# One attention-and-experts kernel: threshold searches over bf16 digits, closer row units, and two output tiles side by side

## Chip, cores and metric

The kernel runs on one NeuronCore of a Trainium2 chip, as one launch. The metric is device time in microseconds (us). The engines are named as the trace names them: PE (matrix products), DVE (VectorE), ACT (ScalarE), POOL (GpSimd), SP (DMA issue).

## What is computed

```python
# attention: q, k, v of [8, 8, 576, 64], tau = 0.02
scores = (q @ k.T) / sqrt(64)
scores = where(scores >= rowmax(scores) - tau, scores, -1e9)
x = softmax(scores) @ v                       # reshaped to [4608, 512]
# routing: 8 experts, 576 places each
flat = (x @ w_gate).flatten(); order = argsort(-flat)
for idx in order:                             # best (token, expert) pair first
    tok, e = divmod(idx, 8)
    if assigned[tok] >= 0 or counts[e] >= 576: continue
    assigned[tok] = e; counts[e] += 1
# experts
for e in range(8): out[assigned == e] = relu(x[assigned == e] @ w1[e]) @ w2[e]
```

## The kernel before

**Attention (0 to about 441 us).** The eight batches pass through scores, threshold softmax (on DVE line 75 takes the row maximum and line 91 applies it; POOL line 76 makes the bias `nb` between the two) and products with `v`. Two batches are also turned at the end: 30 *row units* (`xt_unit`, PE line 247, ACT lines 250 and 251, one DMA each) transpose a tile of `x` and send it to a table `xrows` in DRAM. They use two PSUM banks, `xo0` and `xo1`, in turn. The last loop of `attention` deals them out at a pitch `XTY` between the steps of the first search.

**Routing.** The greedy assignment is made one expert at a time: `Router.phase` finds the threshold at which the next expert fills its 576 places. The 4608 tokens lie as [128 partitions, 36 columns]; `prep` takes each token's best logit `b` and a one-hot of its expert `oh`. Then a *search* of seven steps narrows the threshold. One step is: `step_cmp` on DVE compares all 36 columns with 16 or 32 trial values (128x576 or 128x1152 results, `cmp`); `step_cnt` on PE counts them per expert in nine matmuls (line 500); the counts of four column blocks are added; `step_flag` on DVE (`jka`) sees which trial values still overfill; `step_n` on PE (line 549, later 535) sums the flags, and DVE makes the next trial values from the sum (`jk`, `E`, or `st` and `sd`). How the four blocks are added hangs on the search's number `count`: for 1 and 2 DVE copies (`cn`) and PE adds with four matmuls (line 519); for 3 DVE multiplies and reduces (`cm`, `c8n`) and PE adds with one matmul (line 517); above `ADDS=3` DVE copies and adds three times (`cs`).

After a search, `pick`, `rank1` and `pack` turn the threshold into a list of 576 rows (`gq`, `gx`, `scol`, `poh`, `th`, `R`, `ob`, `idx`; PE lines 591, 592, 619, 625), and POOL gathers these rows of `xrows` by indirect DMA (`xg`, line 798). Search 1 runs alone after attention; search r+2 runs inside the expert stage r.

**Experts (about 489 to 960 us).** Each stage is an FFN on PE in three-term f32r products (high and low parts): first products (line 884, eight tiles f of 128 hidden units, 12 matmuls for each half of the rows), then second products (line 916): five row tiles in the order `L2O=(0,4,1,2,3)`, each over f = 0 to 7. DVE makes the low part of each hidden tile (`H<-hf,H`), of the weights (`w1l`, `w2l`) and of the inputs (`xl`).

**Who sets the order.** All engines' queues are filled by a Python planner when the program is built. The class `Vec` (line 412) keeps an expected time for DVE: 0.07 us plus the elements at 0.96 per ns, or at 1.9 per ns for a `tensor_tensor` whose output and first input are bf16 (line 424, `twice`). PE's matmuls are dealt out at fixed expected pitches, and a step of the search is put into PE's queue when the planner expects DVE to be done. Low-priority DVE work (`H`, `w2l` and others) waits in a list `fills` and is pulled between search steps. Once the program runs, each engine goes through its queue in order and waits wherever the real time differs.

Of the kernel before, what the change touches and what calls it, by code (L numbers as in the profile page):

```python
# [19 lines left out]
PPB=8; LTB=1; VTB=4; HOLD=1; XW=520; NBO=2; NDEF=4; XTB=4; XTY=1.05; XT0=-1.2; XRB=2  # L20


def attention(ctx, tc, qk, vl, wgd, xrows, xts, Lg, nb_batches, ident, dup, idle, R, after_first):
    nc=tc.nc
# [273 lines left out]
    def tail():  # L298
# [89 lines left out]
NC_=36; J=32; CAP=576; BIGS=8192.0; RC=1.5*2.0**28; NH=20; ADDS=3  # L388

def const_arrays():  # L390

    k=np.zeros((128,4096),np.float32); o={}; pos=0
    def put(name,a):
        nonlocal pos
        a=np.asarray(a,np.float32)
        if a.ndim==1: a=np.broadcast_to(a,(128,a.size))
        k[:a.shape[0],pos:pos+a.shape[1]]=a; o[name]=(pos,a.shape[1]); pos+=a.shape[1]
    e=[2.0**(-126+16*i) for i in range(16)]
    put("E1",np.array([-FMAX]+[-x for x in reversed(e)]+e+[FMAX]))
    put("pw",np.array([2.0**i for i in range(J+2)])); put("nw",np.array([2.0**-i for i in range(J+2)]))  # L400
    put("lev",2.0**(1-5.0*np.arange(1,6)))
    lw=np.tile(2.0**(1-5.0*np.arange(1,6)),(128,1)); lw[0,4]=0; put("lew",lw)
    put("io",np.arange(J+2)); put("io4",np.arange(J+2)/16)
# [5 lines left out]
    put("eye",np.eye(128))  # L409
    return k[:,:pos].copy(),o  # L410
# [22 lines left out]
class Router:  # L433
# [8 lines left out]
    def setup(s,ident):  # L442
# [3 lines left out]
        s.eye=t("eyer",[128,128],F32R); V.tensor_copy(s.eye,ident)  # L446
# [5 lines left out]
        x=ident.rearrange("p (c t) -> p c t",c=4); V.tensor_reduce(s.own,x,axis=AX.X,op=ALU.add)  # L452
        with s.nc.allow_low_precision(reason="one term of each sum is not zero"): V.tensor_reduce(s.sum,x.rearrange("p c t -> p t c"),axis=AX.X,op=ALU.add)
    def consts(s):
        V=s.V; G=s.G
        t=lambda n,sh,dt:s.cp.tile(sh,dt,name=n)
        s.tri=t("trib",[128,128],BF16); V.scalar_tensor_tensor(s.tri,s.k("eye"),BIGS,s.k("tri"),op0=ALU.mult,op1=ALU.add)
# [3 lines left out]
        s.cmp=t("cmp",[128,NC_*J],BF16); s.fl=t("fla",[128,6],BF16); G.memset(s.fl,0.0)  # L461
# [49 lines left out]
    def step_flag(s,lv):  # L511
# [3 lines left out]
        else:  # L515
            n=s.ps()[0:32,0:8]
            if s.count>2: s.T.matmul(n,s.sum,s.cn,start=True,stop=True)
            else:
                for c in range(4): s.T.matmul(n,s.eye[:,32*c:32*c+32],s.cn[:,8*c:8*c+8],start=(c==0),stop=(c==3))
        if lv==1: V.tensor_scalar(s.st,s.st,s.lo,None,op0=ALU.add)  # L520
        jk=s.wk.tile([32,9],BF16,name="jka"); s.jk=jk; m=s.js
        fl=jk[:,8:9] if lv==5 else s.fl[0:m,lv+1:lv+2]
        V.tensor_scalar(jk[0:m,0:8],n[0:m],CAP-0.5,None,op0=ALU.is_ge,op1=ALU.max,accum_out=fl)
    def step_n(s,B):

        V=s.V
        lv=B["lv"]
        ps=s.ps()
        if lv>0:


            d=ps[:,0:1]
            for l in range(lv,0 if s.alone else lv-1,-1):
                k=32 if l==5 else 128
                s.T.matmul(d,s.hb[0:k,l-1:l].to_broadcast([k,128]),s.jk[:,8:9] if l==5 else s.fl[:,l+1:l+2],start=(l==lv),stop=(l==1 or not s.alone))
            if not s.alone and lv<5:
                sd=s.wk.tile([128,1],F32,name="sd",bufs=3)
                if lv==1: V.tensor_copy(sd,d)
                else: V.tensor_tensor(sd,B["add"],d,op=ALU.add)
                d=sd  # L540
            if lv<5: return {"add":d,"lv":lv+1}
            s.T.matmul(ps[:,1:10],s.ones[0:32],s.jk,start=True,stop=True)
            lo=s.wk.tile([128,1],F32,name="lo5",bufs=2)
            if s.alone: V.tensor_tensor(lo,s.lo,d,op=ALU.add)
            else: V.scalar_tensor_tensor(lo,d,B["add"],s.lo,op0=ALU.add,op1=ALU.add)
            return {"lo":lo,"lv":6,"full":ps}
        E2=s.wk.tile([128,J+2],F32,name="E",bufs=3)
        n=ps[:,0:1]
        s.T.matmul(n,s.ones,s.fl[:,lv+1:lv+2],start=True,stop=True)
        sm=s.wk.tile([128,2],F32,name="sm",bufs=3); lo=sm[:,0:1]  # L550
        jk=s.wk.tile([128,J+2],F32,name="jk2")
        V.scalar_tensor_tensor(jk,s.k("io"),n,B["E"],op0=ALU.is_equal,op1=ALU.mult,accum_out=lo)
        if lv==-1:

            V.tensor_scalar(E2,s.k("pw"),lo,FMAX,op0=ALU.mult,op1=ALU.min)
            V.scalar_tensor_tensor(E2,s.k("nw"),lo,E2,op0=ALU.mult,op1=ALU.max)
        else:
            s.ab=sm[:,1:2]
            V.scalar_tensor_tensor(s.ab,lo,-1.0,lo,op0=ALU.mult,op1=ALU.max)
            V.tensor_scalar(E2,s.k("io4"),s.ab,lo,op0=ALU.mult,op1=ALU.add)  # L560
        return {"E":E2,"lo":lo,"lv":lv+1}
# [19 lines left out]
    def rank1(s,E):  # L581
# [3 lines left out]
        V.scalar_tensor_tensor(gq[:,:NC_],s.b,lo,gm,op0=ALU.is_gt,op1=ALU.mult)  # L585
# [62 lines left out]
    def phase(s,last=False):  # L648
# [10 lines left out]
        if last:  # L659

            lo=s.wk.tile([128,1],F32,name="lo"); V.memset(lo,-FMAX/4); E={"lo":lo}
        else:
            E={"E":s.k("E1"),"lv":-1}
# [38 lines left out]
GA=[5.0,6.5,8.0,8.0]; AGE=7.0; HALF=1; WARM=[30,6,64]  # L702
W1Y=1.0; W1X=8.5; L2O=(0,4,1,2,3); L2Z=1; HFB=3; RW=[0.2,0.4,0.4,0.4]; LOWP=(); LPF=7; LOWT=1.4; PREPW=1; WLY=(1.0,1.0)

def moe(ctx,tc,R,start,xrows,w1,w2,out,ident):
# [11 lines left out]
    fills=[]  # L717
    def later(k,g): fills.append((clk[0],k,g))
    def pull(k=None):
        if fills:  # L720
            i=next((i for i,x in enumerate(fills) if x[1]==k),None)
            if i is None: i=next((i for i,x in enumerate(fills) if x[1][0] in ("hl","w2l","w2")),0)
            _,k,g=fills.pop(i); g(); done.add(k)
    R.fill=pull
    def flush():
        while True:
            if fills and (clk[0]-fills[0][0]>AGE or (not R.on and V.free<=clk[0]+0.2)): pull()
            yield 0.3

# [128 lines left out]
    def ffn(r,s):  # L858
        H=wk.tile([128,8,2*CAP],F32R,name="H")
        def want(*k):  # L860
            while k not in done:
                if any(x[1]==k for x in fills): pull(k)
                else: yield k

# [196 lines left out]
```

## Time and profile before

| | |
|---|---|
| three runs | 967.71 us median (966.82 to 968.75) |
| the profiled execution | 965.63 us, its span 963.9 us |
| PE busy | 936.5 us (97%) |
| DVE busy | 775.7 us (80%) |
| mean granted TensorE clock | 0.996 |

The span runs from the first to the last instruction of the profiled execution; the device time has 1.7 us around it. Busy shares are averages over stages with different limits, so they have to be read stage by stage. Of a row of the timeline the first number is the start, the second the duration; durations contain the time an instruction spends in the pipeline, so the pitch of a series is read from start to start.

### The profile page before, as it was taken

What the parts mean: (1) busy time and instruction counts of PE and PEld (TensorE: products, weight loads), DVE (VectorE), ACT (ScalarE), POOL (GpSimd) and SP (SyncE); (2) the same over time, 40 slices, a digit from 0 to 9 for tenths busy, and PEclk for the clock granted to TensorE, in tenths of its full rate; (3) what the DMA queues carried; (4) which work ended last, traced back from release to release, by engine and by line L of the source; (5) the groups of instructions that cost most, each with busy time, mean ns of one, the idle gap of its engine ahead of it and who ended that gap; (6) DMA issues with size and microseconds to landing.
All of it is one profiled execution on the core that took longest, in us unless ns stands there. A gap on an engine that the chain in (4) does not pass through costs nothing.

```text
span 963.9 us, 24282 instructions
## 1 busy us (share of the span) xinstructions
PE 936.5 (97%) x9182; PEld 700.8 (73%) x9182; DVE 775.7 (80%) x2177; ACT 638.3 (66%) x1301; POOL 277.7 (29%) x485
## 2 busy tenths in 40 slices
PE   7999999999999999998889999999999999999996
PEld 4565666566566656565778797897988979898994
DVE  8999999999999999996778787788897978536220
ACT  6999999999999999996645343443543525455430
POOL 3434354353534343340020302113041323310101
PEclk9999999999999999999999999999999999999999
DMA  6322252533432333205752505325342516530101
GB/s 260 124 101 88 85 195 93 205 127 111 168 111 101 125 102 123 88 2 193 251 181 74 191 18 173 107 90 175 105 154 94 168 49 215 183 103 32 39 12 44
DMA packets 36293, 117.02 MB, mean 121 GB/s; under 512 B 4304, under 2 KB 4944, under 8 KB 35664
## 3 DMA queue, kind: packets, MB, share of 16 engines
q1 hardware_dynamic: 28784, 93.89, 27.9%
q0 software_dynamic: 5888, 19.03, 6.3%
q10 hardware_dynamic: 1504, 2.54, 0.9%
q8 instruction: 73, 1.20, 0.5%
q14 instruction: 44, 0.36, 0.1%
HBM read 93.01 MB, written 21.38 MB: 119 GB/s over the span
## 4 chain that ended last, share of the span: by engine, by line
PE 84%; DVE 7%; issue 5%; DMA 2%; POOL 0%; ACT 0%; POOLq 0%; ACTq 0%; DVEq 0%
PE pf L884 19%; PE pf L916 18%; PE sc L70 15%; PE xo L156 14%; PE tb L99 9%; PE sc L99 2%; PE xo L166 2%; PE pt L825 1%; DVE cmp L429 1%; DVE z L75 1%; DVE pp L91 1%; PE rps L500 1%; DMA out_dram<-y,idx 1%; PE xo L178 1%; DMA xg<-xrows,idx 1%
## 5 line engine op out<-in xcount | busy, mean ns | idle before, releaser
L75 DVE TENSOR_SCALAR_CACHE_REDUCE z<-sc 128x576 f32<-128x576 f32 x288 | 205.9, 752 | 15.1 <-PE sc L70 13.1
L76 POOL TENSOR_SCALAR nb<-nb,wg 128x1 f32<-128x1 f32 x288 | 144.8, 504 | 248.1 <-DVE z L75 185.5
L87 ACT ACTIVATE pp<-z,nb 128x576 f32<-128x576 f32 x256 | 192.9, 773 | 24.0 <-DVE z L75 20.7
L91 DVE SCALAR_TENSOR_TENSOR pp<-z,nb,pp 128x576 f32<-128x576 f32 x256 | 200.0, 814 | 0.0
L916 PE MATMUL pf<-w2h,H 128*128 128x512 f32 x576 | 191.5, 398 | 1.9 <-DVE H L429 1.9
L70 PE MATMUL sc<-qk 64*128 64x288 f32 (+1 forms) x1280 | 177.8, 421 | 1.0 <-DVE z L75 0.8
L156 PE MATMUL xo<-pt,vt 128*64 128x320 f32 (+1 forms) x1024 | 155.7, 420 | 0.0
L117 ACT ACTIVATE pt<-tb 128x512 f32<-128x512 f32 x253 | 137.7, 591 | 1.9 <-PE tb L99 1.3
L916 PE MATMUL pf<-w2l,H 128*128 128x512 f32 x320 | 128.4, 401 | 0.4 <-DVE w2l L429 0.4
L924 POOL DMA_INDIRECT out_dram<-y,idx x40 | 44.2, 1105 | 289.4 <-ACT y L919 188.0
L916 PEld LDWEIGHTS pf<-w2h,H 128*128 128x128 f32 x576 | 107.4, 189 | 22.4 <-DVE H L429 2.3
L70 PEld LDWEIGHTS sc<-qk 64*128 64x128 f32 (+1 forms) x1280 | 93.1, 177 | 27.9 <-DVE z L75 3.9
L884 PE MATMUL pf<-xl,w1h 128*128 128x288 f32 (+2 forms) x512 | 110.1, 299 | 0.0
L884 PE MATMUL pf<-xh,w1h 128*128 128x288 f32 (+2 forms) x512 | 109.9, 299 | 0.1
L884 PE MATMUL pf<-xh,w1l 128*128 128x288 f32 (+2 forms) x512 | 110.0, 299 | 0.0
L99 PEld LDWEIGHTS tb<-ident,pp 64*128 64x128 f32 x2032 | 75.2, 140 | 44.9 <-issue 18.9
L156 PEld LDWEIGHTS xo<-pt,vt 128*64 128x64 f32 x1024 | 60.7, 136 | 58.4 <-issue 32.4
L919 ACT ACTIVATE y<-pf 128x512 f32<-128x512 f32 x40 | 23.9, 598 | 117.2 <-PE pf L916 111.7
L896 ACT ACTIVATE hf<-pf 128x576 f32<-128x576 f32 x56 | 36.5, 653 | 89.4 <-PE pf L884 83.5
L99 PE MATMUL tb<-ident,pp 64*128 64x64 f32 x2032 | 91.9, 227 | 3.3 <-ACT pt L117 3.0
L798 POOL DMA_INDIRECT xg<-xrows,idx x40 | 51.1, 1278 | 132.3 <-PE pf L884 45.7
L884 PEld LDWEIGHTS pf<-xh,w1h 128*128 128x128 f32 x512 | 81.8, 188 | 1.0 <-ACT xh L826 0.3
(206 smaller groups left out, 1358.2 us busy)
## 6 DMA issues: line engine op xcount, KB each, us to landing
qk<-qk_dram SPq DMA_DIRECT2D x31, 864.0 KB, 4.5
vt<-vl_dram SPq DMA_DIRECT2D x32, 576.0 KB, 3.7
w2s<-w_dram SPq DMA_DIRECT2D x32, 512.0 KB, 5.5
w1s<-w_dram SPq DMA_DIRECT2D x28, 512.0 KB, 5.8
xrows<-pp SPq DMA_DIRECT2D x24, 260.0 KB, 2.3
xts<-xt SPq DMA_DIRECT2D x2, 1152.0 KB, 5.6
pt<-xts SPq DMA_DIRECT2D x2, 1152.0 KB, 6.9
xrows<-xr SPq DMA_DIRECT2D x8, 260.0 KB, 2.2
```

The lines of the kernel that those rows point to most:

```text
L70: T.matmul(sc[o,f,:HS], kd["q",h][r,c], kd["k",h][r,:],start=True,stop=True)
L75: V.tensor_scalar(z,SC.pop(t)[:,:,:HS],-0.125,None,op0=ALU.mult,op1=ALU.min,accum_out=nb[:,0:1])
L76: G.tensor_scalar(nb[:,1:2],nb[:,0:1],taub[:,0:1],None,op0=ALU.add)
L87: A.activation(pview(t),ZB[t].rearrange("p a b -> p (a b)"),AF.Exp,bias=NBI[t][:,0:1],scale=-1.0)
L91: V.scalar_tensor_tensor(pv,ZB.pop(t).rearrange("p a b -> p (a b)"),NBI[t][:,1:2],pv,op0=ALU.is_le,op1=ALU.mult,accum_out=den_of(p)[:,p%4/ ...
L99: g=slice(64*r,64*r+64); T.transpose(o[:,r],x[r%len(x)][g],ident[g,g])
L117: else: A.activation(o,tb,AF.Copy)
L156: T.matmul(xo[64*h:64*h+64,:q.stop-q.start],v[:,f,128*u+64*h:128*u+64*h+64],PT[p][:,h,u,q],start=new,stop=last,skip_group_check=True)
L798: G.indirect_dma_start(out=x[:n],out_offset=None,in_=xrows,in_offset=IOA(ap=s["idx"][:n,t:t+1],axis=0))
L884: T.matmul(ps[:,h,:n],s[w][:,k,f*128:(f+1)*128],s[x][:,k,cols[h]],start=(i==0),stop=(i==11))
L916: T.matmul(ps[:,0,:],H[:,f,c:c+128],s[w][:,f],start=(f==0 and j==0),stop=e)
L924: G.indirect_dma_start(out=out,out_offset=IOA(ap=s["idx"][:n,t:t+1],axis=0),in_=y[:n],in_offset=None)
```

## The change

1. **Digits.** `Router.digits` turns each best logit into an ordered integer and cuts it into seven digits `D` (5, 5, 5, 5, 4, 4, 4 bits), bf16: six new DVE operations per search. A step compares the running value `e` with constants `th`, bf16 against bf16; the next `e` is one operation on 128x36. The steps have 32, 32, 32, 32, 16, 16, 16 trial values; before 32, 16, 16, 32, 32, 32, 32.
2. **Two layouts.** Search 1 writes `cmp` as (group, trial value, 4 columns), the innermost four contiguous in every operand. Searches 2 to 7 write it as (column, trial value): innermost, `e` is a broadcast and `th` is read every fourth element.
3. **ADDS = 1.** Searches 2 and 3 add the four count blocks on DVE (`cs`) as the later ones did; lines 519 and 517 lose their matmuls there.
4. **Row units** at a pitch of 0.9 in place of 1.05.
5. **Constants.** POOL makes `th`, the powers `unit` and the shifts `sh` in `consts`.
6. **Second products.** Tiles t=0 and t=4 are begun together: t0 with f 0 to 6, t4 with f 0 to 5, then t0 with f 7, then t4 with f 6 and 7. `fills` are pulled by a due time.

```diff
-PPB=8; LTB=1; VTB=4; HOLD=1; XW=520; NBO=2; NDEF=4; XTB=4; XTY=1.05; XT0=-1.2; XRB=2
+PPB=8; LTB=1; VTB=4; HOLD=1; XW=520; NBO=2; NDEF=4; XTB=4; XTY=0.9; XT0=-1.2; XRB=2
-        R.prep(0,31); R.compare(R.k("E1"),J,0,31)
+        R.prep(0,31); R.compare(0,31)
         both_ev(b,x[:,:,384:],slice(0,64),V); V.tensor_copy(rd[64:128,:,4],RD[b-1][64:128,:,4])
+        for g in R.digits(0,31): g()
-NC_=36; J=32; CAP=576; BIGS=8192.0; RC=1.5*2.0**28; NH=20; ADDS=3
+NC_=36; J=32; CAP=576; BIGS=8192.0; RC=1.5*2.0**28; NH=20; ADDS=1
+SHL=(0,5,10,15,20,24,28); SHR=(27,)*4+(28,)*3; JS=(32,)*4+(16,)*3; NL=7
...
+        G.iota(s.th[0],pattern=[[1,32],[0,4]],base=1,channel_multiplier=0,allow_small_or_imprecise_dtypes=True)
+        for l in range(NL):
+            G.memset(s.unit[:,l:l+1],64.0**-l)
+            for i,n in enumerate((SHL[l],SHR[l])): G.memset(s.sh[:,i,l:l+1],n)
+            if l: G.tensor_scalar(s.th[l],s.th[0][:,:JS[l]],64.0**-l,-64.0**-l if l==NL-1 else 0.0,op0=ALU.mult,op1=ALU.add)
...
+    def digits(s,c0=0,c1=NC_):
...
+        return [lambda: V.tensor_scalar(z,s.b[:,c0:c1],0.0,None,op0=ALU.add),
+            lambda: V.tensor_scalar(k,zi,31,-2**31,op0=ALU.arith_shift_right,op1=ALU.bitwise_or),
+            lambda: V.tensor_tensor(k,zi,k,op=ALU.bitwise_xor),
+            lambda: V.tensor_tensor(d,k.unsqueeze(1).to_broadcast([128,NL,n]),w(s.sh[:,0]),op=ALU.logical_shift_left),
+            lambda: V.tensor_tensor(d,d,w(s.sh[:,1]),op=ALU.logical_shift_right),
+            lambda: V.tensor_tensor(D,d,w(s.unit),op=ALU.mult)]
...
+    def step_cmp(s,l):
+        V=s.V; s.js=m=JS[l]
+        if s.alone and l==0: s.compare(31); return
+        e=s.e if l else s.D[:,0]
+        if s.count>ADDS: V.tensor_tensor(s.cmp.rearrange("p (c j) -> p c j",j=J)[:,:,:m],e.unsqueeze(2).to_broadcast([128,NC_,m]),s.th[l][:,:,0].unsqueeze(1).to_broadcast([128,NC_,m]),op=ALU.is_ge)
+        else: V.tensor_tensor(s.cmp.rearrange("p (g j c) -> p g j c",j=J,c=4)[:,:,:m],e.rearrange("p (g c) -> p g c",c=4).unsqueeze(2).to_broadcast([128,9,m,4]),s.th[l].unsqueeze(1).to_broadcast([128,9,m,4]),op=ALU.is_ge)
...
+            s.T.matmul(n,u,s.fl[0:m,l:l+1],start=True,stop=True)
+            e=s.wk.tile([128,NC_],BF16,name="e0",bufs=3)
+            V.scalar_tensor_tensor(e,s.e if l else s.D[:,0],n,s.D[:,l+1],op0=ALU.subtract,op1=ALU.add)
...
+            if not s.alone: work(6)
...
-        for t in L2O:
-            ps=pf.tile([128,2,512],F32,name="pf")
...
+        two=L2O[:2]
+        for t,fs in zip(two,(range(7),range(LATE))): yield from prods(t,fs)
+        for t,fs in zip(two,((7,),range(LATE,8))): yield from prods(t,fs); yield from leave(t)
+        for t in L2O[2:]: yield from prods(t,range(8)); yield from leave(t)
```

**Where instructions move, first place:** DVE in FFN 1, from the last operations of `prep` for search 3 to the hidden tiles that the second products wait for. `z`, `key`, `dg` and `D` are the digits. Before:

```order
L429 TENSOR_TENSOR oh<-q,qm 128x288
L429 CAST ob<-cps 128x160
L429 TENSOR_TENSOR cmp<-b,cst 128x1152
L429 TENSOR_TENSOR H<-hf,H 128x512
L429 TENSOR_TENSOR H<-hf,H 128x64
```

Now:

```order
L426 TENSOR_TENSOR oh<-q,qm 128x288
L426 CAST ob<-cps 128x160
L426 TENSOR_SCALAR z_9746<-b 128x36
L426 TENSOR_SCALAR key<-z_9746 128x36
L426 TENSOR_TENSOR key<-z_9746,key 128x36
L426 TENSOR_TENSOR dg<-key,sh 128x252
L426 TENSOR_TENSOR dg<-dg,sh 128x252
L426 TENSOR_TENSOR D<-dg,unit 128x252
L426 TENSOR_TENSOR cmp<-D,th_599 128x1152
L426 TENSOR_TENSOR H<-hf,H 128x512
L426 TENSOR_TENSOR H<-hf,H 128x64
```

Six operations have come in between `ob` and the compare, and two hidden tiles (f 6 and f 7) instead of one now stand behind the compare.

**Second place:** PE at the same moment, second products of FFN 1. Nine rows of the count (line 500, now 516) follow each other; one is shown. Before:

```order
L916 MATMUL pf<-w2l,H 128x512
L916 MATMUL pf<-w2h,H 128x512
...
L916 MATMUL pf<-w2h,H 128x512
L916 MATMUL pf<-w2l,H 128x512
L916 MATMUL pf<-w2h,H 128x512
L916 MATMUL pf<-w2l,H 128x512
L500 LDWEIGHTS cmp
```

Now:

```order
L614 MATMUL cps<-ob,zz 128x10
L918 MATMUL pf<-w2h,H 128x512
L516 LDWEIGHTS cmp
L516 MATMUL rps<-oh,cmp 128x32
...
L918 MATMUL pf<-w2h,H 128x512
L918 MATMUL pf<-w2l,H 128x512
L918 MATMUL pf<-w2h,H 128x512 x2
L918 MATMUL pf<-w2l,H 128x512
```

Before, five second products stand between the 16 matmuls on `ob` (line 625) and the count; now one does, and the products over f 6 and those of tile t=4 stand behind the count.

**Third place:** PE in FFN 1 between the flag sum of a step (line 535, now 543) and the count of the next (line 500, now 516), a step in the middle of search 3. Before:

```order
L535 MATMUL rps<-fla,hb 128x1
L884 MATMUL pf<-xl,w1h 128x288 x2
L884 MATMUL pf<-xh,w1l 128x288 x2
L884 MATMUL pf<-xh,w1h 128x288 x2
L884 MATMUL pf<-xl,w1h 128x288 x2
L884 MATMUL pf<-xh,w1l 128x288 x2
L884 MATMUL pf<-xh,w1h 128x288 x2
L884 MATMUL pf<-xl,w1h 128x288 x2
L884 MATMUL pf<-xh,w1l 128x288 x2
L500 LDWEIGHTS cmp
```

Now:

```order
L543 MATMUL rps<-fla,unit 128x1
L884 MATMUL pf<-xl,w1h 128x288 x2
L884 MATMUL pf<-xh,w1l 128x288 x2
L884 MATMUL pf<-xh,w1h 128x288 x2
L884 MATMUL pf<-xl,w1h 128x288 x2
L884 MATMUL pf<-xh,w1l 128x288 x2
L884 MATMUL pf<-xh,w1h 128x288 x2
L516 LDWEIGHTS cmp
```

Sixteen first products stood between the two; now twelve.

## Rows read from the trace of the kernel before

**Rows 1.** Three stretches of the span: attention, FFN 0 and most of FFN 1, and the change from FFN 1 to FFN 2. Columns: length; busy time of PE, PE's weight loads, DVE, ACT and POOL; granted TensorE clock; DMA share; GB/s.

```profile
0.00:441.00 441.00, 435.60 (x5478) 264.60 (x5478) 421.78 (x1186) 410.53 (x818) 179.18 (x397) 1.00 0.35 121
...
489.00:581.00 92.00, 90.77 (x719) 80.96 (x720) 76.27 (x211) 45.21 (x102) 11.23 (x11) 1.00 0.34 110
581.00:597.00 16.00, 14.14 (x85) 10.80 (x84) 11.77 (x36) 4.93 (x9) 4.98 (x5) 0.89 0.56 184
```

**Rows 2.** What PE waited for longest between 489 and 959 us: in total, times, longest.

```profile
PE pf L916 <- DVE H L429: 1.9, 1, 1.9
```

**Rows 3.** Search 1 in the timeline: two compares on DVE, one step apart, then PE's first count and its last.

```profile
461.61 1.42 DVE L429 SCALAR_TENSOR_TENSOR cmp<-st,sc,b 128x1152 bf16<-128x1152 f32 x1 [0.39 <-PE sc L535]
...
464.64 1.42 DVE L429 SCALAR_TENSOR_TENSOR cmp<-st,sc,b 128x1152 bf16<-128x1152 f32 x1 [0.38 <-PE sc L535]
...
450.74 0.21 PE L500 MATMUL sc<-oh,cmp 128*128 128x32 bf16 x2 [0.34 <-DVE cmp L429]
...
469.21 0.39 PE L500 MATMUL sc<-oh,cmp 128*128 128x32 bf16 x9 [0.20 <-DVE cmp L429]
```

**Rows 4.** Two row units that follow each other on ACT, in the timeline (the small copy of line 251 between them is left out).

```profile
456.06 0.59 ACT L250 ACTIVATE pp<-xo 64x512 f32<-64x512 f32 x1
...
456.75 0.60 ACT L250 ACTIVATE pp<-xo 128x512 f32<-128x512 f32 x1
```

**Rows 5.** Groups of DVE instructions from 489 to 959 us: busy time, mean ns of one, idle time before them.

```profile
L429 DVE TENSOR_TENSOR cmp<-b,E 128x576 bf16<-128x576 f32 x12 | 9.1, 757 | 0.3
L429 DVE TENSOR_TENSOR cmp<-b,cst 128x1152 bf16<-128x1152 f32 x5 | 6.8, 1351 | 0.0
L429 DVE TENSOR_TENSOR poh<-pio,prb 128x1152 bf16<-128x1152 bf16 x7 | 5.3, 754 | 0.0
L429 DVE TENSOR_TENSOR oh<-q,qm 128x288 bf16<-128x288 bf16 x6 | 2.7, 458 | 0.2
L429 DVE TENSOR_TENSOR q<-q,w8b 128x288 bf16<-128x288 bf16 x6 | 1.8, 307 | 0.2
L429 DVE SCALAR_TENSOR_TENSOR gm<-qm,m,ge 128x36 bf16<-128x36 bf16 x7 | 1.7, 246 | 0.0
L429 DVE TENSOR_SCALAR r<-scol 128x36 f32<-128x36 f32 x7 | 1.3, 183 | 0.2
```

**Rows 6.** FFN 0, second step of search 2, in the timeline: DVE, then PE.

```profile
493.75 0.25 DVE L429 SCALAR_TENSOR_TENSOR jk<-cst,rps 128x34 f32<-128x34 f32 x1
...
494.50 0.75 DVE L429 TENSOR_TENSOR w1l<-w1s,w1h 128x256 fp32r<-128x256 f32 x2
...
495.98 0.39 PE L500 MATMUL rps<-oh,cmp 128*128 128x32 bf16 x9 [0.84 <-DVE cmp L429]
...
496.88 0.27 PE L519 MATMUL rps<-cn,eyer 128*32 128x8 f32 x4
497.01 0.54 PE L884 MATMUL pf<-xh,w1h 128*128 128x320 f32 x2
```

**Rows 7.** FFN 1, a step of search 3, in the timeline: PE, then DVE.

```profile
567.68 0.17 PE L517 MATMUL rps<-c8n,sum 128*32 128x8 f32 x1
...
568.06 0.43 PE L884 MATMUL pf<-xl,w1h 128*128 128x288 f32 x2
568.33 0.43 PE L884 MATMUL pf<-xh,w1l 128*128 128x288 f32 x2
568.60 0.18 PE L535 MATMUL rps<-fla,hb 128*128 128x1 bf16 x1
...
569.02 1.42 DVE L429 SCALAR_TENSOR_TENSOR cmp<-st,sd,b 128x1152 bf16<-128x1152 f32 x1
```

**Rows 8.** From FFN 1 to FFN 2, in the timeline: DVE, then PE.

```profile
579.77 0.31 DVE L429 TENSOR_TENSOR_SCAN gx<-onesb,gq 128x72 bf16<-128x72 bf16 x1
...
587.15 0.32 DVE L429 CAST ob<-cps 128x160 bf16<-128x160 f32 x1
587.38 1.35 DVE L429 TENSOR_TENSOR cmp<-b,cst 128x1152 bf16<-128x1152 f32 x1
588.65 0.82 DVE L429 TENSOR_TENSOR H<-hf,H 128x512 fp32r<-128x512 f32 x2
...
583.21 0.62 PE L916 MATMUL pf<-w2h,H 128*128 128x512 f32 x2
...
585.25 0.84 PE L619 MATMUL cps<-R,poh 128*128 128x160 bf16 x9
...
589.39 0.50 PE L916 MATMUL pf<-w2h,H 128*128 128x512 f32 x1 [1.86 <-DVE H L429]
589.73 0.59 PE L625 MATMUL cps<-ob,zz 128*128 128x10 bf16 x16
```

**Rows 9.** POOL's constants in attention and the `nb` behind them, then the DVE operation that needs the first of these `nb`, in the timeline.

```profile
35.41 0.09 POOL L461 MEMSET fla<- 128x6 bf16 x1
35.47 0.39 POOL L463 IOTA pio<- 128x128 bf16 x1
35.94 0.30 POOL L464 TENSOR_SCALAR pio<-pio 128x128 bf16<-128x128 bf16 x1
...
37.01 1.17 POOL L76 TENSOR_SCALAR nb<-nb,wg 128x1 f32<-128x1 f32 x2
...
39.32 0.81 DVE L91 SCALAR_TENSOR_TENSOR pp<-z,nb,pp 128x576 f32<-128x576 f32 x1
```

More of the change, by code (lines that the diff above doesn't have):

```diff
@@ L397, in put @@
         k[:a.shape[0],pos:pos+a.shape[1]]=a; o[name]=(pos,a.shape[1]); pos+=a.shape[1]
[L398 to L403, printed above, removed]
+    top=[(n<<27)^(1<<31) if n>=16 else ~(n<<27)&0xffffffff for n in range(1,32)]
+    put("E0",np.append(np.array(top,np.uint32).view(np.float32),np.finfo(np.float32).max))
     put("w8",8-np.arange(8))
@@ L451, in setup @@
         s.own=t("own",[128,4],F32); s.sum=t("sum",[128,32],F32R)
[L452 to L453 removed]
+        V.tensor_reduce(s.own,x.rearrange("p j c -> p c j"),axis=AX.X,op=ALU.add)
+        with s.nc.allow_low_precision(reason="one term of each sum is not zero"): V.tensor_reduce(s.sum,x,axis=AX.X,op=ALU.add)
     def consts(s):
@@ L518, in step_flag @@
             else:
-                for c in range(4): s.T.matmul(n,s.eye[:,32*c:32*c+32],s.cn[:,8*c:8*c+8],start=(c==0),stop=(c==3))
-        if lv==1: V.tensor_scalar(s.st,s.st,s.lo,None,op0=ALU.add)
+                for c in range(4): s.T.matmul(n,s.eye[:,c],s.cn[:,8*c:8*c+8],start=(c==0),stop=(c==3))
         jk=s.wk.tile([32,9],BF16,name="jka"); s.jk=jk; m=s.js
-        fl=jk[:,8:9] if lv==5 else s.fl[0:m,lv+1:lv+2]
+        fl=jk[0:m,8:9] if l==NL-1 else s.fl[0:m,l:l+1]
         V.tensor_scalar(jk[0:m,0:8],n[0:m],CAP-0.5,None,op0=ALU.is_ge,op1=ALU.max,accum_out=fl)
[L524 to L561, printed above, removed]
@@ L659, in phase, with work @@
         if last:
-            lo=s.wk.tile([128,1],F32,name="lo"); V.memset(lo,-FMAX/4); E={"lo":lo}
+            lo=s.wk.tile([128,1],F32,name="lo"); V.memset(lo,-FMAX/4); E={"v":s.b,"lo":lo}
         else:
-            E={"E":s.k("E1"),"lv":-1}
+            todo=s.digits(31 if s.alone else 0)
+            def work(n):
+                while n and todo: todo.pop(0)(); n-=1
+            if not s.alone: work(6)
             def gap():
@@ L715, in moe, with due, later @@
     done=set()
-    fills=[]
-    def later(k,g): fills.append((clk[0],k,g))
+    fills=[]; ready={}; l1s={}
+    def due(k):
+        r=k[1]; t=l1s.get(r)
+        if k[0]=="hl": return clk[0]+min(8.0,3.35*(7-k[2])+0.68*k[2]+0.5)
+        if k[0] in ("w2l","w2"): return (clk[0]+8.0 if t is None else t+27.5)+0.68*(k[2] if len(k)>2 else 7)
+        if k[0]=="y5": return clk[0]+AGE
+        t=l1s.get(r-1); late=k[0]=="w1a" or k[0]=="w1p" and k[2]==1
+        return (clk[0]+20.0 if t is None else t+55.0)+(12.0 if late else 0.0)
+    def later(k,g): fills.append((clk[0],k,g,due(k)))
     def pull(k=None):
@@ L721, in pull @@
             i=next((i for i,x in enumerate(fills) if x[1]==k),None)
-            if i is None: i=next((i for i,x in enumerate(fills) if x[1][0] in ("hl","w2l","w2")),0)
-            _,k,g=fills.pop(i); g(); done.add(k)
+            if i is None: i=min(range(len(fills)),key=lambda i:fills[i][3])
+            _,k,g,_=fills.pop(i); g(); done.add(k); ready[k]=V.done
     R.fill=pull
@@ L726, in flush @@
         while True:
-            if fills and (clk[0]-fills[0][0]>AGE or (not R.on and V.free<=clk[0]+0.2)): pull()
+            if fills and (clk[0]-fills[0][0]>AGE or min(x[3] for x in fills)<max(V.free,clk[0])+DUE or (not R.on and V.free<=clk[0]+0.2)): pull()
             yield 0.3
@@ L863, in want @@
                 else: yield k
+            if l2 and ready.get(k,0.0)>clk[0]: yield ready[k]-clk[0]
         blocks=[(f,(0,1)) for f in range(8)]
```

93 lines of the change are left out of this document (54 added, 39 removed).

## The prediction, made before the changed kernel ran

> **What bounds the kernel now.** First the table of stretches [rows 1]: attention is held by two engines at once, PE busy for 435.60 of 441 us and DVE for 421.78, so that anything late on DVE there has little slack to vanish in. From 489 us on the FFNs follow each other on PE, and PE hardly waits: 1.9 us for a hidden tile `H` [rows 2] and 0.84 us for a compare [rows 6] are the two waits of any size. A change in the FFNs can therefore win only by taking work off PE, or by removing those two waits; it can lose by making PE wait at places where it doesn't now. Between the two lies search 1, a chain with nothing beside it but the row units: its steps follow each other every 3.03 us [rows 3], and 1.42 us of that is the compare. The sum below is made against the profiled execution, 965.63 us, which is 2.1 us under the median of the three runs; the same change is then put on the median, 967.71 us.
>
> **How fast the new compares are.** Everything hangs on this. No row shows a bf16 compare, but three bf16 operations on DVE stand near it [rows 5]. `poh` on 128x1152 has four contiguous elements innermost in its operands and takes 0.754 us; the f32 compare of the same size takes 1.351. `q<-q,w8b` on 128x288, contiguous, takes 0.307 us. `oh<-q,qm`, the same size and type, but with one operand repeated along the innermost direction, takes 0.458: the bf16 type alone gave it nothing. Search 1's new layout is that of `poh`, so I take 0.754 us for its wide compares, and for the narrow ones about half of that and the fixed part, 0.46. The layout of searches 2 to 7 is that of `oh` (a repeated `e`, and `th` at every fourth element), so I take the f32 prices, 1.35 wide and 0.757 narrow; the other end is 0.75 and 0.46. The Trainium skill, "VectorE: DVE Perf Modes", section "What auto-detection actually checks", says that the double rate of a two-source operation wants every tensor 16 bits wide with a step of one. By that rule the compares of searches 2 to 7 gain nothing from bf16, and the trace agrees (0.458 against 0.307 us). If the rule did not hold here, the time would be that of the first rival.
>
> **Part by part.**
>
> *A, constants on POOL: +0.6 us (0 to +1.5).* `consts` gets 21 more small memsets, one iota and six scalings. Start to start a memset is 0.06 us, an iota 0.47, a 128x128 scaling 0.26 [rows 9], a 128x64 one between 0.06 and 0.26, say 0.16: 1.26 + 0.47 + 0.78 + 0.48 = 3.0 us, put ahead of the `nb` that start at 37.01. The first of these would be ready near 40.4, and DVE wants it at 39.32 [rows 9]: 1.1 us late, and the next operations in DVE's queue wait behind it. DVE is idle for 4% of this stage, so part may be made up later; I take half. Next late is nothing: POOL is otherwise idle for most of attention.
>
> *B, search 1: -1.9 us (-0.9 to -3.4).* From the first count to the last it takes 469.21 - 450.74 = 18.47 us now [rows 3]. A wide step becomes 3.03 - 1.42 + 0.75 = 2.36, and 0.25 more since the next value `e` is now an operation of its own (priced as `gm`, 0.246 [rows 5]): 2.61. A narrow one becomes 2.3. Three of each are 14.8 us, a gain of about 3.4 with the shorter end. But row units stand between the steps' matmuls in PE's queue: 5, 3, 4, 4, 3 and 4 of them in the six steps, and ACT empties one bank in 0.69 us, start to start [rows 4]. The steps with 5 and 4 units then last 3.45 and 2.76 us, those with 3 keep 2.6 and 2.3: 16.7 us in all, a gain of 1.8, and 0.1 at the end. The last row units also end earlier, so the gather and FFN 0 move with it. The digits of most columns lie in the tail of attention, the last ones beside the first step. If the new layout ran at the f32 rate, the gain would be 0.9.
>
> *C, FFN 0: +1.0 us (+0.2 to +1.8).* In search 2 the sum of the first step lets DVE begin at 493.75 [rows 6]. Now follow `e` (0.25), one piece of `w1l` (half of 0.75) and the wide compare (1.35): the count can start at 495.75, against 495.98. But the planner believes the compare to be short, and puts 1.0 us less of first products (some 1.4 us instead of 2.4) in front of the count. PE is there earlier and waits 0.84 + 1.0 - 0.2 = 1.6 us. The next step adds 0.2. The six digits of search 2 themselves cost nothing: they lie where DVE and PE wait for the first gathered rows.
>
> *D, FFN 1 to FFN 2: +0.9 us (-0.5 to +2.0).* Now PE waits 1.86 us, until 589.39, for `H` of the last tile, which stands on DVE behind the compare that starts at 587.38 [rows 8]. The two row tiles side by side should hide this. The order says otherwise: the count of search 3 stands in PE's queue after only 18 second products, and f 6 and f 7 both stand on DVE behind the compare. From `gx` at 579.77 DVE reaches the end of `ob` after 7.7 us [rows 8]; then six digits (three as `r`, 0.183, three near `oh`, 0.458 [rows 5]: 1.9) and the compare: 10.9. PE from the same point: 0.4 to its answer, 20 first products at 0.133 (a pair every 0.27 [rows 7]) 2.7, 18 second products at 0.227 (nine between 583.21 and 585.25 [rows 8]) 4.1, `L619` 0.64 and `L625` 0.5: 8.3. It waits 2.6, and perhaps 0.1 more for f 6: 2.7 instead of 1.86. That the granted clock is 0.89 of full over these 16 us [rows 1] (some 3.5 us at 1.2 GHz, a cost of 1.8) stays, since the wait before it stays.
>
> *E, steps of searches 3 to 7: +1.6 us (0 to +3.0).* From the flag sum to the next compare's start DVE needs 0.42 us, the compare 1.42 [rows 7]; with `e` and 1.35 it is again 1.9 us, narrow 1.3. PE had 2.2 us of products there. Now it has 12 instead of 16 in the place shown, 1.6 us and 0.1 around them: a wait of 0.2. Over the six gaps of FFN 1 (1.42, 1.60, 1.60 wide; 1.06, 1.33, 1.06 narrow, by the pitch of the products in the order) I get 0.9, in FFN 2 0.35, later 0.2; and 0.15 for pieces of `w1l` that DVE is busy with when the sum comes.
>
> *F, matmuls taken off PE: -2.2 us.* `L517` and the pair behind it take 0.38 us (567.68 to 568.06) where a pair takes 0.27 [rows 7]: 0.11 each. `L519` takes 0.13 [rows 6] and the same 0.07 behind it: 0.20. Seven of each go: 2.2 us. The three additions on DVE are no later than the way through PE was.
>
> The sum is 0.6 - 1.9 + 1.0 + 0.9 + 1.6 - 2.2 = 0.0: 965.6 us profiled, **967.7 us** as a median. The new order of `fills` and the moves of `y5` and `z` are taken at nothing: they lie on DVE and ACT beside PE's products; without that cover each would cost one wait like those in E.
>
> **Rivals.** *1. All compares run at the double rate (faster).* Then a step needs 1.3 us, C falls to +0.2, D to +0.3, E to 0, and the sum is 0.6 - 1.9 + 0.2 + 0.3 - 2.2 = -3.0: 964.7; with the whole 3.4 of B 963.2. For it: the planner counts so. Against it: `oh`. *2. FFN 0's wait brings the clock down (slower).* It decides if the wait in C reaches the 1.86 us after which the clock fell once: C at its upper end (2.4 us of wait) does. The price is 1.8 us for the half clock and 0.8 for C: 970.3. For it: the one wait of that size in the FFNs was followed by half clock. Against it: after the 0.84 us wait it was not (1.00 from 489 to 581 us [rows 1]), and my value is 1.6. *3. Search 1 doesn't get shorter.* The banks of the row units hold the steps at some 3 us; B is near 0, the result 969.5. Against it: now there are three or four units to a step of 3.03 us, and ACT is idle between them. *4. The change doesn't do in the second products what it says*: that is in the forecast, D.
>
> **How the numbers follow.** The forecast has a chance of 0.42, with a range of its own of 965 to 970.5; rival 1 0.28, rival 2 0.18, rival 3 0.12. About 0.2% (1.9 us) is what a measurement of this kernel can tell from no change, so faster means under 965.8 and slower over 969.6. Faster: rival 1 but for 0.02, and 0.09 of the forecast, where B or D are at their good ends: 0.35. Slower: rival 2 but for 0.03, half of rival 3, 0.07 of the forecast: 0.28. The same: 0.37. The range takes in rival 1 to its far end and rival 2 with A at its upper end: 963.0 to 971.5.
>
> **What would show it.** Compares of searches 2 to 7 at 1.35 and 0.76 us, of search 1 at 0.75 and 0.46. First to last count of search 1 in 16.7 us. PE's waits in the FFNs at 6 to 7 us in all, the longest, about 2.7 us, for the first compare of search 3, with half clock behind it. An idle DVE of about 1 us near 39 to 41 us. The prediction is wrong if compares in the FFNs take 0.75 us, if the wait at FFN 2 is gone, or if PE's waits come to over 9 us.

## The result: slower by 0.7%

The changed kernel takes 975.38 us (median of six runs, 975.20 to 976.03); six runs of the kernel before beside it had a median of 968.5, so the ratio is 1.0069 (95% interval 1.0052 to 1.0086). The forecast was no change, 967.7 us in a range of 963.0 to 971.5. The profiled execution has a span of 973.6 us where the kernel before had 963.9. From one start of a stage to the next, by the first product of each kind in the two timelines:

| stretch | before | changed | difference |
|---|---|---|---|
| attention, to the last logit product | 446.66 | 449.15 | +2.5 |
| search 1 to the first product of FFN 0 | 42.16 | 40.92 | -1.2 |
| FFN 0 | 63.24 | 63.51 | +0.3 |
| FFN 1 | 63.95 | 66.74 | +2.8 |
| FFN 2 | 59.42 | 63.24 | +3.8 |
| FFN 3 | 58.64 | 61.51 | +2.9 |
| FFN 4 and 5 | 115.67 | 114.49 | -1.2 |

FFN 6 and 7 have no search beside them and are unchanged.

What PE waited for in the FFNs of the changed kernel (489 to 972 us: total, times, longest):

```profile
PE rps L516 <- DVE cmp L426: 5.6, 5, 2.0
PE rps L543 <- DVE jka L426: 0.8, 1, 0.8
PE pf L884 <- DVE xl L426: 0.2, 1, 0.2
```

That is 6.6 us, where the forecast had 6 to 7, and the longest, 2.0 us, is the wait that it named. (The section on the change, the prediction and some expectations call this compare the first of search 3. By their own numbering it opens search 4: in the trace of before the seven counts of search 3 start from 538.74 to 575.41 us, and the first count of search 4 at 591.34. It is called so from here on.) The kernel before waited 3.1 us in its FFNs, so the waits alone don't carry the loss: PE is also *busy* for longer, 467.96 us instead of 462.11 between 489 and 972 us, though it has fewer matmuls (3205 instead of 3222). The timeline of PE in FFN 2 shows where, a step of search 4:

```profile
623.30 0.43 PE L884 MATMUL pf<-xl,w1h 128*128 128x288 f32 x2
623.58 0.42 PE L884 MATMUL pf<-xh,w1l 128*128 128x288 f32 x2
623.93 0.17 PE L543 MATMUL rps<-fla,unit 16*128 16x1 bf16 x1
624.03 0.54 PE L884 MATMUL pf<-xh,w1h 128*128 128x288 f32 x2
624.41 0.43 PE L884 MATMUL pf<-xl,w1h 128*128 128x288 f32 x2
```

Compare the step in [rows 7]. There the flag sum has the form 128*128 and starts 0.27 us after the pair ahead of it. Here its form is 16*128 (16 rows of operands, 128 columns): it starts 0.35 us after the pair, and the next product 0.10 us after it, where a sum of 128 rows leaves 0.04 (the rows of e1_rows128 below show it); from the pair behind it to the next one it is 0.38 us, where it is 0.35 there. Together some 0.17 us for a sum of one column. The change had cut the operands of `step_n` to the `m` rows that carry trial values.

DVE in attention, and POOL ahead of it:

```profile
36.31 0.39 POOL L461 IOTA th<- 128x128 bf16 x1
...
37.55 0.74 POOL L465 TENSOR_SCALAR th<-th 128x128 bf16<-128x128 bf16 x1
...
41.88 2.03 POOL L76 TENSOR_SCALAR nb<-nb,wg 128x1 f32<-128x1 f32 x4
...
42.20 0.82 DVE L91 SCALAR_TENSOR_TENSOR pp<-z,nb,pp 128x576 f32<-128x576 f32 x1 [1.94 <-POOL nb L76]
```

The first `nb` behind the constants starts at 41.88 instead of 37.01 [rows 9], and DVE waits 1.94 us for it. Of these 4.87 us, 0.83 are a later start (POOL's `w8b` ahead of the constants begins at 35.21 instead of 34.38); the new constants take 4.0 us, where the forecast had 3.0.

Search 1, a wide compare on DVE, PE's first count and its last; then the wide compares and `e` of the later searches, mean ns:

```profile
458.56 0.76 DVE L426 TENSOR_TENSOR cmp<-e,th 128x1152 bf16<-128x1152 bf16 x1
...
453.15 0.38 PE L516 MATMUL sc<-oh,cmp 128*128 128x32 bf16 x9
...
470.04 0.38 PE L516 MATMUL sc<-oh,cmp 128*128 128x32 bf16 x9
```
```profile
L426 DVE TENSOR_TENSOR cmp<-D,th 128x1152 bf16<-128x1152 bf16 x5 | 6.8, 1358 | 0.2
L426 DVE SCALAR_TENSOR_TENSOR e<-e,rps,D 128x36 bf16<-128x36 bf16 x30 | 7.8, 259 | 15.2 <-PE rps L543 15.0
```

Search 1 runs its bf16 compares at the double rate (0.76 against 1.42 us in [rows 3]) and passes from first to last count in 16.89 us; in searches 2 to 7 the same comparison takes 1.358, as the f32 one did [rows 5].

From FFN 1 to FFN 2, DVE and PE:

```profile
587.76 0.32 DVE L426 CAST ob<-cps 128x160 bf16<-128x160 f32 x1
...
590.02 1.36 DVE L426 TENSOR_TENSOR cmp<-D,th 128x1152 bf16<-128x1152 bf16 x1
...
588.95 0.48 PE L918 MATMUL pf<-w2h,H 128*128 128x512 f32 x1
591.43 0.39 PE L516 MATMUL rps<-oh,cmp 128*128 128x32 bf16 x9 [2.00 <-DVE cmp L426]
```

The wait for `H` [rows 8] has become one for the count, 2.00 us instead of 1.86. No half clock followed it in this execution.

### The profile page after: what moved, and what is told of

Its sections match the earlier page's. It is cut to its first block, busy times and chain, and to the rows that moved or that the text cites. A ratio compares the mean times of both kernels' runs of the same rounds, so it can differ in the third digit from the quotient of the medians.

```text
span 973.6 us, 24239 instructions
## 1 busy us (share of the span) xinstructions
PE 943.0 (97%) x9137; PEld 700.4 (72%) x9137; DVE 776.6 (80%) x2203; ACT 640.5 (66%) x1301; POOL 278.0 (29%) x513
## 4 chain that ended last, share of the span: by engine, by line
PE 78%; DVE 11%; issue 6%; DMA 2%; ACT 1%; POOL 1%; POOLq 0%; DVEq 0%
PE pf L884 18%; PE pf L918 16%; PE sc L70 14%; PE xo L156 13%; PE tb L99 8%; PE sc L99 2%; DVE cmp L426 2%; DVE z L75 2%; PE xo L166 1%; PE xo L247 1%; DVE pp L91 1%; DVE xl L426 1%; PE pt L824 1%; PE rps L516 1%; PE xo L178 1%
## 5 line engine op out<-in xcount | busy, mean ns | idle before, releaser
L921 POOL DMA_INDIRECT out_dram<-y,idx x40 | 40.6, 1016 | 311.2 <-ACT y L924 198.9
```

## Experiments

Theory R: the flag sums over 16 and 32 rows hold up PE. Theory D: PE's waits for DVE, whose compares run slower than the planner counts. The experiments ran in four sets, each on one chip, with the kernel before beside them; its median lay between 964.2 and 968.1 in these sets and at 968.5 beside the result. So ratios are compared within a set, and the spans of the profiled executions beside them. The sets are: e1 to e4; after_again, e7, e9 and e13; b1, e17, e18 and e19; e20, e21 and e22. In the spans, stretches of 3.4 us at half clock (1.2 GHz instead of 2.4) fall into some executions of one kernel and not into others; each costs up to 1.7 us.

**e1_rows128**, flag sums over all rows.

```diff
-s.fl=t("fla",[32,NL-1],BF16)
+s.fl=t("fla",[128,NL-1],BF16)
...
-s.T.matmul(n,u,s.fl[0:m,l:l+1],start=True,stop=True)
+s.T.matmul(n,u,s.fl[:,l:l+1],start=True,stop=True)
```

> The changed kernel, with every flag sum of the search (lines 543, 547, 548) taken over all 128 rows, the unused rows zero, instead of over the 16 or 32 rows that carry trial values; same order of instructions. Theory R (a matmul of 16 or 32 rows between products of 128 rows makes PE finish the one before it and restart: in the changed kernel's trace the product before it takes 0.227 instead of 0.133 us or 0.321 instead of 0.227, the sum itself 0.10 instead of 0.04, the product behind it 0.02 more): 0.17 us for each of 42 sums or pairs of sums in the FFNs, so 7 us less, 968.3. Theory D (the time went into PE's waits for DVE, whose compares run at the f32 rate while the planner counts them at the double rate): unchanged, 975.4.

970.77 us, ratio to before 1.0074 (1.0057 to 1.0090), span 968.3 (changed: 973.6). PE in the timeline:

```profile
620.79 0.42 PE L884 MATMUL pf<-xh,w1l 128*128 128x288 f32 x2
621.06 0.18 PE L543 MATMUL rps<-fla,unit 128*128 128x1 bf16 x1
621.10 0.51 PE L884 MATMUL pf<-xh,w1h 128*128 128x288 f32 x2
621.45 0.43 PE L884 MATMUL pf<-xl,w1h 128*128 128x288 f32 x2
```

Theory R: the sum is back to 0.27 and 0.04 us, 5.3 us of span are gone. PE is busy for 7.1 us less from 489 to 972 us (467.96 to 460.91); its waits grew from 6.6 to 8.2, since it now reaches them earlier. The ratio doesn't show the gain: the changed kernel did not run in this set, and the kernel before was 4.3 us faster in it than beside the result.

**e2_before_rows32**, the reverse: the kernel before with its sums over 32 rows.

```diff
-k=32 if l==5 else 128
+k=32
...
-s.T.matmul(n,s.ones,s.fl[:,lv+1:lv+2],start=True,stop=True)
+s.T.matmul(n,s.ones[0:32],s.fl[0:32,lv+1:lv+2],start=True,stop=True)
```

> The kernel before, with its flag sums over 32 rows instead of 128 (the other rows hold zeros there, so the sums are the same), all else as it was. Theory R: 36 sums in the FFNs at 0.17 us, 6 us more, 974.5. Theory D: unchanged, 968.5.

970.71 us beside 964.18, ratio 1.0077 (1.0058 to 1.0096): 6.5 us more by the medians, with nothing else changed. Its PE:

```profile
565.92 0.42 PE L884 MATMUL pf<-xh,w1h 128*128 128x288 f32 x2
566.28 0.17 PE L535 MATMUL rps<-fla,hb 32*128 32x1 bf16 x1
566.38 0.53 PE L884 MATMUL pf<-xl,w1h 128*128 128x288 f32 x2
566.75 0.42 PE L884 MATMUL pf<-xh,w1l 128*128 128x288 f32 x2
```

PE's waits are those of the kernel before (1.8, 0.8, 0.4 us). Theory D plays no part in this pair: theory R is shown in time here, and in the spacing of the rows in both experiments.

**e3_spread**, POOL's new constants in eight pieces.

```diff
 if (b,j)==(0,0): queue.append(("n",lambda: True,False,R.consts,p))
+elif 1<=p<=8: queue.append(("n",lambda: True,False,lambda: R.parts.pop(0)(),p))
```

> The changed kernel, with POOL's new constants (th, unit, sh) made in eight pieces over the next eight head pairs of attention instead of in one go. If the 1.94 us for which DVE waits for nb at 42.2 us is lost for good: 1.9 us less, 973.5. If it was made up later in attention: unchanged, 975.4.

974.76 us, ratio 1.0112 (1.0094 to 1.0130), span 973.6. DVE's wait is gone, and the last logit product comes at 447.71 instead of 449.15; this execution had two half-clock stretches between 484 and 491 us that the one of the changed kernel did not have, and gave the 1.4 us back. So the stage shows the gain, the total doesn't.

**e4_price**, the planner told the f32 rate for those compares.

```diff
-twice=n=="tensor_tensor" and out.dtype==BF16 and ins[0].dtype==BF16
+twice=n=="tensor_tensor" and out.dtype==BF16 and ins[0].dtype==BF16 and not s.slow
...
+V.slow=s.count>ADDS
```

> The changed kernel, with the planner told that the compares of searches 2 to 7 run at 0.96 elements per ns, so that it puts more products between a flag sum and the next count. Theory D: the waits of 1.5, 1.1, 0.3, 0.7 us behind compares go (the 2.0 us at FFN 2 stays, since the digits stay): 2.5 to 3.5 us less, 972.4; if nearly all of the loss were such waits, 969. Theory R: not more than those 3 us, since the sums of 16 and 32 rows stay.

979.55 us, ratio 1.0159 (1.0139 to 1.0180), span 977.6: slower than e3 in the same set. The waits:

```profile
PE rps L545 <- DVE jka L426: 3.7, 3, 2.2
PE rps L518 <- DVE cmp L426: 2.8, 3, 1.6
PE pt L826 <- DVE cs L426: 0.8, 1, 0.8
```

Waits behind compares halve, as expected, and turn up behind `jka` and `cs`. Behind two of them, of 1.6 us at 617 and 2.2 at 665, PE ran at half clock for 6.8 and 3.4 us. The true price for one operation doesn't make a better plan; this expectation failed.

**after_again, e7_rows_spread, e9_rows_spread_adds7, e13_rows_spread_seq**: the changed kernel, then both mends; then all searches in the fast layout with PE adding the blocks (`ADDS=7`); then the second products one tile after the other.

```diff
-for t,fs in zip(two,(range(7),range(LATE))): yield from prods(t,fs)
-for t,fs in zip(two,((7,),range(LATE,8))): yield from prods(t,fs); yield from leave(t)
-for t in L2O[2:]: yield from prods(t,range(8)); yield from leave(t)
+for t in L2O: yield from prods(t,range(8)); yield from leave(t)
```

> The changed kernel once more, beside the next three on the same chip, so that their differences from it can be read without the difference between two chips. Expected 973.6 us of span, 975 us.

> The changed kernel with both mends: flag sums over all 128 rows, and POOL's new constants in eight pieces. Theory R and the constants account for 5.3 + 1.3 us of span: 967.0 of span, 968.7 us, still 3 us over the kernel before, and what is left then lies in PE's waits in the FFNs (8 to 9 us where the kernel before had 3).

> As e7_rows_spread, with ADDS=7: searches 2 to 7 take the layout of search 1, so their compares have four contiguous elements innermost (0.76 and 0.46 us), and their count blocks are added by PE (line 517 or 519) instead of DVE. Theory D (what is left is waits behind compares at the f32 rate): the waits behind compares fall by 0.6 us each, 3 us in all, against 0.11 to 0.20 us of PE for each of 35 steps in place of none, 4 us, less what DVE's three additions held up: between 2 us less and 2 us more than e7_rows_spread, with PE's waits at 4 us. Rival (the waits come from where the planner puts the steps, whatever the compares take): PE's waits stay near 8 us and the time rises by 4 us.

> As e7_rows_spread, with the second products one row tile after the other as before the change. If side by side helped: 0.5 to 2 us more, since f 6 and f 7 of tile 0 then stand behind the compare of search 3. If it only moved the wait (the count of search 3 is the first to wait, at FFN 2, either way): unchanged within 0.5 us.

| | us | ratio to before (interval) | span |
|---|---|---|---|
| after_again | 975.78 | 1.0083 (1.0066 to 1.0100) | 974.4 |
| e7_rows_spread | 972.15 | 1.0053 (1.0033 to 1.0074) | 969.8 |
| e9_rows_spread_adds7 | 970.33 | 1.0038 (1.0015 to 1.0061) | 968.6 |
| e13_rows_spread_seq | 969.74 | 1.0019 (1.0006 to 1.0032) | 968.5 |

The two mends win 3.6 us by the medians (the intervals of the ratios still touch), and are not all of it: e7 is still slower than the kernel before. A part of what they win comes back as half clock. (1 - granted clock) x span, averaged over a kernel's runs, estimates the time lost to it: 4.6 us for after_again, 7.4 for e7, 7.1 for e13 and 4.9 for the kernel before; 2 to 4 us of each lie at the end, when PE is done. The fast layout of e9 brings PE's waits from 7.7 to 6.2 us, not to the 4 expected, and puts the sums of 42 steps on PE; as a whole it can't be told from e7. One tile after the other is 2.4 us better than side by side, which neither branch of the expectation had.

**b1_pitch**, the kernel before with `XTY=0.9` alone; **e17_search_alone**, e13 with the fills in the old order too; **e19** and **e18**, the same with `ADDS=3` and 7.

```diff
...
-i=min(range(len(fills)),key=lambda i:fills[i][3])
+i=next((i for i,x in enumerate(fills) if x[1][0] in ("hl","w2l","w2")),0)
...
```

> The kernel before, with the row units at a pitch of 0.9 in place of 1.05 and nothing else. If the row units held search 1: up to 1 us less, 967. If the f32 compares set its steps: unchanged or, with three more row units between its matmuls, up to 0.5 us more.

> The changed search (digits, two layouts, ADDS=1, row units closer) with both mends (flag sums over 128 rows, constants in eight pieces), but the second products and the fills' order as in the kernel before. If the rest of the loss lay in the new order of the fills: PE's waits in the FFNs fall from 8 to 4 us and the time to 966. If it lies in the digits and f32-rate compares of searches 2 to 7: within 1 us of e13_rows_spread_seq, span 968, PE's waits at 7 to 8 us.

> As e17_search_alone with ADDS=3: searches 2 and 3 have the double-rate layout and PE adds their blocks. The waits behind compares of searches 2 and 3 (1.6 us in FFN 0, 0.5 in FFN 1) fall by 0.6 us a step, 1.5 to 2 us in all, against 2.2 us more of matmuls: within 1 us of e17_search_alone by time, with PE's waits 2 us shorter.

> As e17_search_alone with ADDS=7: all searches in the double-rate layout, all blocks added by PE. PE's waits behind compares nearly gone but for the first compare of search 3 (2 us less 0.6), 4 us in all; 35 steps with 0.11 to 0.20 us more of matmuls, 4.5 us: within 1 us of e17_search_alone.

Ratios: b1 1.0012 (1.0000 to 1.0024), e17 0.9993 (0.9979 to 1.0007), e19 1.0010 (0.9996 to 1.0025), e18 1.0018 (1.0004 to 1.0033). With the old plan for the fills and both mends the new search is level with the old one, though PE's waits fell only to 6.4 us and not to 4. Putting more searches into the fast layout doesn't help. In e18 the waits behind compares fall from 4.8 to 2.6 us, but PE is busy for 3.7 us more from 489 to 972 us, in part at half clock behind a new wait of 2.1 us for `c8n`; e19 has a wait of 3.6 us for the third compare of search 4, until 597.61, and 6.8 us at half clock from 597 on. Closer row units do nothing good by themselves: with the f32 compares search 1 takes 19.83 us from first to last count in b1's trace, instead of 18.47.

**e21_side_oldfill** (e17 with side by side), **e22_price_oldfill** (e17 with the f32 price) and **e20_yield** (e17 with the digits in three pairs):

```diff
-if not s.alone: work(6)
+if not s.alone:
+    for i in range(3): work(2); yield V.ease()
```

> As e17_search_alone, with the second products' first two row tiles side by side, but the fills pulled in the old order. With e7, e13 and e17 this makes four kernels from two switches. If the fills' order by due time costs the 2.5 us between e13 and e17: this is within 1 us of e17_search_alone. If the side by side costs too, as e7 against e13 has it (2.4 us by the medians, 1.3 us by the spans): 1 to 2.5 us more than e17.

> As e17_search_alone, with the planner told the f32 rate for the compares of searches 2 to 7. With the fills' order by due time the true price cost 4 us (e4_price). If that came from the due times, which the longer search upsets: here the waits behind compares (1.6, 0.5, 1.1, 0.6 us) shrink and the time falls by 1 to 2 us. If a search that the planner spreads further loses elsewhere: unchanged or up to 3 us more.

> As e17_search_alone, with the six digits of searches 2 to 7 given to the planner in three pairs, between which it may place hidden tiles: at FFN 2 the last hidden tile now stands on DVE ahead of the digits and the compare instead of behind them. If that place is what PE waits for: the 1.6 us wait for H goes and 1 to 1.6 us with it, 964.5, under the kernel before. If the first compare of search 3 takes over: a wait of 1 us or more for it instead, and no gain.

e21 1.0019 (1.0010 to 1.0028), e22 1.0063 (1.0050 to 1.0077), more than either branch of its expectation. Two switches, four kernels, ratio to before:

| | fills by due time | fills in the old order |
|---|---|---|
| side by side | 1.0053 | 1.0019 |
| one tile after the other | 1.0019 | 0.9993 |

Each switch costs 0.26 to 0.34%, some 2.5 to 3.3 us, whichever way the other stands. Only the two kernels of the left column ran in one set, where their intervals just don't overlap. The fills' order is compared across sets alone, and there the ratios themselves may move by as much: e3, the changed kernel without one wait, has 1.0112 in its set, the changed kernel 1.0069 and 1.0083. So the price of side by side is shown, that of the fills' order is likely. The lost clock points the same way: an estimated 7.4 and 7.1 us in the left column, 4.7 and 5.3 in the right one. In the profiled executions PE waits 2.00 us for the compare in e7 and e13, until 589.36 and 589.11, and runs at half clock to 593; in e17 and e21 it waits 1.60 us for `H` in that place, at full clock. e22 fails like e4: 2.7 us of wait until 614.81, and 6.8 us at half clock from 614 on.

e20 is the one that beats the kernel before: **963.09 us**, ratio 0.9978 (0.9968 to 0.9988). But not where it was expected. PE still waits 1.4 us for `H` ahead of FFN 2. Its interval overlaps that of e17 (0.9979 to 1.0007, another set), so what the digits' places win over e17 is read from the traces. The gain lies ahead of FFN 0, which starts 37.9 us after the last logit product instead of 40.5. PE there in e17, then in e20:

```profile
481.77 0.42 PE L518 MATMUL rps<-oh,cmp 128*128 128x32 bf16 x9 [2.41 <-DVE cmp L427]
482.03 2.93 PE L638 MATMUL cps<-trib,onesb 128*128 128x128 bf16 x26
484.98 0.63 PE L826 MATMUL pt<-ident,xg 128*128 128x128 f32 x4
```
```profile
480.21 1.61 PE L638 MATMUL cps<-trib,onesb 128*128 128x128 bf16 x26
482.95 0.63 PE L828 MATMUL pt<-ident,xg 128*128 128x128 f32 x4 [1.12 <-DVE xg L427]
```

In e17 the first count of search 2 stands in PE's queue ahead of the transposes of the gathered rows, and waits 2.41 us for the six digits and the compare; then the 26 matmuls run in part at half clock. In e20 the planner, given a choice between the digits, puts that count behind the transposes. The chain of work that ended last says the same: up to the transposes it runs through the digits and the compare to the count in e17 and in the changed kernel, through the gather's DMA in e20 and in the kernel before.

## Why the prediction was wrong

*F failed.* "Matmuls taken off PE: -2.2 us" counted what goes, and put the sums of `step_n` at nothing, as the same instruction under another line number. They had lost rows. The price stood in the trace of before, in rows that the forecast did not draw: the old search's last two sums had 32 rows,

```profile
577.44 0.43 PE L884 MATMUL pf<-xh,w1l 128*128 128x288 f32 x2
577.80 0.17 PE L535 MATMUL rps<-jka,hb 32*128 32x1 bf16 x1
577.84 0.16 PE L542 MATMUL rps<-jka,onesb 32*128 32x9 bf16 x1
577.93 0.53 PE L884 MATMUL pf<-xh,w1h 128*128 128x288 f32 x2
```

0.36 us from the pair to the sum instead of 0.27, and 0.13 to the next product. There are 36 such sums in the FFNs now, beside six pairs that were of this kind before: 36 x 0.17 is 6 us, and e2 measured 6.5. Two sums of 32 rows in a row (577.80, 577.84) stand 0.04 apart, so it is the step between forms that costs, on both sides. The Trainium skill, "TensorEngine Tiling (Array Packing)", section "Key Properties", says that changing the tiling mode drains the engine; the trace agrees for sums of few rows, and puts about 0.17 us on there and back. It shows no such price for sums with all rows and few columns, form 128*32:

```profile
567.42 0.42 PE L884 MATMUL pf<-xh,w1l 128*128 128x288 f32 x2
567.68 0.17 PE L517 MATMUL rps<-c8n,sum 128*32 128x8 f32 x1
567.72 0.51 PE L884 MATMUL pf<-xh,w1h 128*128 128x288 f32 x2
```

This one starts 0.26 us after the pair and leaves 0.04, as a sum of 128*128 does. So by these traces it is the rows that cost; that a drain is the reason isn't measured.

*A was mis-sized:* 1.94 us of wait, not 0.6. The three large scalings took 0.31 to 0.74 us where one row had given 0.30 (why isn't shown), and little of the wait was made up: without it the last logit product of e3 came 1.4 us earlier. Most of the rest of attention's 2.5 us is a later start: DVE's first row maximum comes at 5.68 instead of 4.93 us, in e3 too. In e17_search_alone it comes at 4.93 and the last logit product at 446.57, so this part comes and goes.

*B was right as a chain* (16.89 us against 16.7 from first count to last; the steps with narrow compares last 2.73, 2.51 and 2.68 us, hardly less than the wide ones' 3.49, 2.74 and 2.74, so row units, not compares, set most of them) *and too large at its end:* -1.2 us up to FFN 0. Its far end of 3.4 us doesn't follow from its steps: 18.47 - 14.8 is 3.7. *C was right in its wait* (1.49 us against 1.6) *and wrong in one sentence:* the digits of search 2 were to cost nothing, since all waited for gathered rows. With search 1 earlier the rows came earlier too, and the digits were what PE's queue waited for; e20 puts 2.6 us on that, 1.3 of them half clock.

*D:* the wait moved to the first compare, as the order said, with 2.0 us instead of 2.7; no half clock came behind it this time. *E:* the rates were as forecast (1.36 and 0.76 us), the places not. The steps of search 3 show no wait; 2.9 us of waits stand at the second and third step of search 4 (1.05 and 0.34) and in search 5 (0.80 and 0.69), where 1.6 in all was forecast. That all waits together came to the forecast's 6 to 7 us is partly luck: with the sums at their old price, in e1, they come to 8.2.

*Taken at nothing:* the order of the fills. By the four kernels above it costs 2.5 to 3.3 us, which no single set shows, and side by side, priced in D by its wait alone, as much again, which one set shows. Which waits they lengthen is shown only for the place at 589 us, since every switch shifts the whole plan. Rival 1 is out (1.358 us), rival 2 didn't come (full clock from the FFNs' start to 968 us), rival 3 didn't either.

Of the 9.7 us between the two profiled executions (6.9 by the medians): the sums' rows are 5 to 7, the constants 1.4 to 1.9, fills and side by side by the estimate above 5 to 6, against which stand 1.7 us of half clock that this execution was spared, the earlier search 1, and 1.2 us in FFN 4 and 5. There the last search ends sooner, 40 us into FFN 4 instead of 58; that this is the reason isn't shown. These sizes are not additive: PE freed in one place waits in the next (e1: 7.1 us less busy, 5.3 us less span).

## What to carry to other kernels

When an instruction keeps its line and its job but changes its shape, look for the new shape in the old trace and price it with what stands before and behind it: a one-column sum over 16 rows cost 0.17 us more than one over 128, four times the 0.04 that the latter leaves to the next start. A count of removed matmuls says nothing until the remaining ones have been compared form by form. And work that hides under a wait stops hiding when the same change shortens that wait.

## What the hardware did that was not expected

A matmul over 16 or 32 rows between products over 128: 0.08 to 0.09 us more ahead of it, 0.06 more to the next start, 0.02 to 0.03 behind that one; 16 and 32 rows the same. A matmul over 128 rows and 32 columns in the same place: nothing more. The same 128x128 scaling on POOL took between 0.30 and 0.74 us. Half clock comes after idle PE in some executions and not in others at the same place: e1 and the changed kernel waited 2.0 us for the first compare of search 4 without it, e7 and e13 with the same wait had it.
